# Decode attention with a parallel MLP on one core: tiles of eight heads in three slots instead of four heads in double buffers

## The chip, the cores and the metric

The kernel runs on one core of a Trainium2 chip. The metric is the device time in microseconds of one launch. A core has five engines with instruction streams of their own: PE (matmul), DVE (vector), ACT (scalar), POOL and SP; SP does no arithmetic here and issues the large loads. Engines meet only at semaphores: an instruction that waits holds up everything behind it in its own stream.

## The reference, cut to what matters

There are 8 sequences with one new token each, 32 heads of 128 and a cache of 4096 keys a head, all in bf16. With `xn` the layer norm of `x`:

```
q = xn @ wq                                   # 8 x 4096, 32 heads of 128
scores = einsum(q, k_cache) * 128**-0.5       # 8 x 32 x 4096
o = einsum(softmax(scores), v_cache)          # 8 x 32 x 128
out = x + o @ wo + gelu(layernorm(xn) @ w1 + b1) @ w2 + b2
```

K and V are 268 MB each; all weights together are some 15 MB. Every byte is used once.

## The kernel before, in words

A tile is one sequence and four heads (`HS = 4`): 4 MB of K and 4 MB of V, so there are 64 tiles. Partition `p` holds 128 consecutive keys of one head, 32 KB in one piece; 32 partitions belong to a head. K and V have two buffers each (`K_sb`, `V_sb`), and a third area `W_sb` holds in turn `wq`, the MLP's weights and `wo`.

Of a tile's 128 key columns, 40 are scored on PE (`jp_of`): groups of eight are transposed (`pe_T`, into `TR_ps`), copied out by ACT (`act_T`, into `KT_sb`) and multiplied by q (`pe_QK`). DVE scores the other 88 in four chunks (`dve_chunk`): multiply by q, add the halves, reduce. `act_S` brings PE's scores beside DVE's, `dve_max` forms one maximum, and `act_exp` takes four exps, one a head, each on that head's 32 partitions; the columns of `P_sb` that belong to other heads' partitions are zero from a memset. `pe_RS` sums the denominators, `pe_PV` runs 128 matmuls, one per key column, with V as the stationary operand, and `act_O` and `o_norm` store the tile's four heads in `oT_sb`.

The order of each engine's work is written out by hand: `at(pos, fn, ...)` notes a call with a position, the list is sorted by position and, at equal positions, by the order of the notes, and each call then appends its instructions to the streams of its engines. Tile `i` owns the positions from 100i to 100i+100, and nothing is reordered later. All five streams are replayed in full, without loops. SP's stream per tile:

```python
            if i >= 2:
                at(o - 90, load_k, i)
            if i >= 1:
                at(o + 20 if i != NQ - 2 else o + 20, load_v, i)
```

`load_k(i)` waits until tile i-2 has been scored (`kt`, `km`), `load_v(i)` until tile i-2's PV is done. At the end, heads 0 to 27 of the output are transposed into a layout that lets `wo` come in large rows (`pe_ot`, `cp_ot`, `pe_ox`, `cp_ox`); the last projection has the attention output as the stationary operand and `wo` moving (`fin_woa`, `fin_wob`). Every operation goes through one replay helper, so the profile gives L99 for nearly all of them, and tiles tell them apart.

Of the kernel before, what the change touches and what calls it, by code (L numbers as in the profile page):

```python
# [13 lines left out]
P = 128  # L14
# [127 lines left out]
def bass_parallel_sum__gqa_block_cached__mixer_channel_mlp__decode_kernel(  # L142
# [16 lines left out]
    assert DH == P and D % P == 0 and B == 8 and H % 4 == 0 and SK % P == 0  # L159
    HS = 4  # L160
# [9 lines left out]
    CHMAX = 22  # L170
    LOOP0, LOOPN = 4, 28
    NHA = H - HS
    assert NKEY == 128
    NS = 5

    def jp_of(i):
        return 64 if i == NQ - 1 else 48 if i == NQ - 2 else 40

    def chunks(i):
        jd = NKEY - jp_of(i)  # L180
        n = -(-jd // CHMAX)
        return [(jd * c // n, jd * (c + 1) // n) for c in range(n)]

    bank0 = [0]
    for i_ in range(NQ):
        bank0.append(bank0[-1] + jp_of(i_) // TPB)
    chunk0 = [0]
    for i_ in range(NQ):
        chunk0.append(chunk0[-1] + len(chunks(i_)))
    V_CUT = {NQ - 2: (0, 64, 128), NQ - 1: (0, 48, 96, 128)}  # L190
    K_CUT = {}
    WO_CUT = (0, 14, 21, 25, 27, NHA)

    x2 = A_x.rearrange("b s d -> (b s) d")
    out2 = out.rearrange("b s d -> (b s) d")

    with ExitStack() as es:
# [5 lines left out]
        K_sb = sb("K_sb", [P, 2, NKEY, DH], BF)  # L203
        V_sb = sb("V_sb", [P, 2, NKEY, DH], BF)
        W_sb = sb("W_sb", [P, DC * H * DH], BF)
        wq_sb = W_sb[:, :].rearrange("p (c n) -> p c n", c=DC)
        w1_sb = W_sb[:, 0:DC * F].rearrange("p (c n) -> p c n", c=DC)
        w2_sb = W_sb[:, DC * F:DC * F + (FB + 1) * D].rearrange("p (c n) -> p c n", n=D)
        woa_sb = W_sb[:, 0:NHA * D].rearrange("p (c n) -> p c n", n=D)
        wob_sb = W_sb[:, NHA * D:H * D].rearrange("p (h n) -> p h n", n=D)  # L210
        O_sb = W_sb[0:B, 0:NHA * DH]
        b1_sb = W_sb[0:1, DC * F + (FB + 1) * D:DC * F + (FB + 1) * D + F]
        assert DC * F + (FB + 1) * D + F <= DC * H * DH and H * D <= DC * H * DH
        KT_sb = sb("KT_sb", [P, NS, TPB, P], BF)
        Y_sb = sb("Y_sb", [P, CHMAX, DH], BF)
        Y2_sb = sb("Y2_sb", [P, 2, CHMAX, DH // 2], BF)
        Sd_sb = sb("Sd_sb", [P, 2, NKEY], F32)
        P_sb = sb("P_sb", [P, 2, NKEY, HS], BF)
# [5 lines left out]
        oX_sb = sb("oX_sb", [P, NHA, B], BF)  # L224
        x_sb = sb("x_sb", [B, D], BF)
        b2_sb = sb("b2_sb", [1, D], BF)
        xn_sb = sb("xn_sb", [B, D], BF)
        y_sb = sb("y_sb", [B, D], BF)
        st_sb = sb("st_sb", [B, 2, 16], F32)
        xT_sb = sb("xT_sb", [P, 2, DC, B], BF)  # L230
        hT_sb = sb("hT_sb", [P, FB + 1, B], BF)
        iota_i = sb("iota_i", [P, P], I32)
        ident_f = sb("ident_f", [P, P], F32)
        ident_bf = sb("ident_bf", [P, P], BF)
        ones_sb = sb("ones_sb", [1, B], BF)
        zeros_sb = sb("zeros_sb", [P, P], BF)
        mx_sb = sb("mx_sb", [P, 32], F32)
        mxT_sb = sb("mxT_sb", [P, 32], F32)
        mq_sb = sb("mq_sb", [P, 1], F32)
        nsc_sb = sb("nsc_sb", [P, 32], F32)  # L240
        mb_sb = sb("mb_sb", [P, 32], F32)
        NB_sb = sb("NB_sb", [P, 2, 32], F32)
        rs4_sb = sb("rs4_sb", [P, 2, HS], F32)
        ri4_sb = sb("ri4_sb", [P, 2, HS], F32)
        ones_f = sb("ones_f", [P, P], F32)
        resT_sb = sb("resT_sb", [P, DC * B], F32)
        out_sb = y_sb
# [3 lines left out]
        PV_ps = ps("PV_ps", [P, 2, 512], F32)  # L251
        CH_ps = ps("CH_ps", [P, 512], F32)
        ACC_ps = ps("ACC_ps", [P, 512], F32)
        TRF = TR_ps[:, :, :].bitcast(F32)
        TRB, SB_, PVB = [_Bank(), _Bank()], [_Bank(), _Bank()], [_Bank(), _Bank()]
        CHB, ACCB = _Bank(), _Bank()
        RS_ps = CH_ps[:, 0:2 * HS].rearrange("p (s h) -> p s h", h=HS)
        QT_ps = CH_ps[:, 64:64 + H * B]
        HT_ps = CH_ps[:, 64:64 + (FB + 1) * B]
        OR_ps = ACC_ps[:, :].bitcast(BF)  # L260
        FIN_ps = S_ps

        pe, dve, act, sp, pool = (_Eng(sem(f"{n}_s")) for n in ("pe", "dve", "act", "sp", "pool"))
        NPIECE = 4
        ld_k = [[_Dma(sem(f"ld_k{s}_{q}")) for q in range(NPIECE)] for s in range(2)]
        ld_v = [[_Dma(sem(f"ld_v{s}_{q}")) for q in range(NPIECE)] for s in range(2)]
        ld_x, ld_b1, ld_b2, ld_wq, ld_w1, ld_w2a, ld_w2b, ld_wob, st_a, st_b = (
            _Dma(sem(n)) for n in ("ld_x", "ld_b1", "ld_b2", "ld_wq", "ld_w1", "ld_w2a", "ld_w2b",
                                   "ld_wob", "st_a", "st_b"))
        ld_woa = [_Dma(sem(f"ld_woa{q}")) for q in range(len(WO_CUT) - 1)]  # L270
# [6 lines left out]

# [3 lines left out]
        def cuts(kind, i):  # L281
            c = (K_CUT if kind == "k" else V_CUT).get(i, (0, NKEY))
            return list(zip(c[:-1], c[1:]))

        def piece_of(kind, i, lo, hi):
            return [tk[(kind, i, q)] for q, (a, b) in enumerate(cuts(kind, i)) if a < hi and b > lo]

        def cache_src(cache, i, lo, hi):
            hq, b = divmod(i, B)
            return cache[b, hq * HS:(hq + 1) * HS].rearrange(  # L290
                "h (p j) d -> (h p) j d", j=NKEY)[:, lo:hi, :]

        def load_k(i):
            s = i % 2
            if i >= 2:
                sp.wait(tk[("kt", i - 2)], tk[("km", i - 2)])
            for q, (lo, hi) in enumerate(cuts("k", i)):
                tk[("k", i, q)] = ld_k[s][q].sig(sp.dma_start(
                    K_sb[:, s, lo:hi, :], cache_src(A_k_cache, i, lo, hi)))

        def load_v(i):
            s = i % 2
            if i >= 2:
                sp.wait(tk[("pv", i - 2)])
            for q, (lo, hi) in enumerate(cuts("v", i)):
                tk[("v", i, q)] = ld_v[s][q].sig(sp.dma_start(
                    V_sb[:, s, lo:hi, :], cache_src(A_v_cache, i, lo, hi)))

        def load_mlp():
            sp.wait(tk["q_all"])  # L310
            tk["b1"] = ld_b1.sig(sp.dma_start(b1_sb, B_b1.rearrange("(o f) -> o f", o=1)))
            tk["w1"] = ld_w1.sig(sp.dma_start(w1_sb, B_w1.rearrange("(p c) f -> p c f", c=DC)))
            tk["w2a"] = ld_w2a.sig(sp.dma_start(
                w2_sb[:, 0:FB, :], B_w2[0:FB * P, :].rearrange("(p c) n -> p c n", c=FB)))
            tk["w2b"] = ld_w2b.sig(sp.dma_start(w2_sb[0:FLAST, FB, :], B_w2[FB * P:F, :]))

        def load_woa(q):
            sp.wait(tk["ox"])
            lo, hi = WO_CUT[q], WO_CUT[q + 1]
            tk[("woa", q)] = ld_woa[q].sig(sp.dma_start(  # L320
                woa_sb[:, lo:hi, :], A_wo[0:NHA * DH, :].rearrange("(p c) n -> p c n", c=NHA)[:, lo:hi, :]))

        def load_wob():
            sp.wait(tk["ox"])
            tk["wob"] = ld_wob.sig(sp.dma_start(
                wob_sb, A_wo[NHA * DH:H * DH, :].rearrange("(h p) n -> p h n", p=P)))


        def consts_pool():
            tk["iota"] = pool.sig(pool.iota(iota_i[:, :], [[1, P]], base=0, channel_multiplier=-1))  # L330
            pool.memset(zeros_sb[:, :], 0.0)
            pool.memset(ones_sb[:, :], 1.0)
            pool.memset(mx_sb[:, :], 0.0)
            pool.memset(rs4_sb[:, :, :], 0.0)
            pool.memset(ones_f[:, :], 1.0)
            t = pool.sig(pool.memset(nsc_sb[:, :], -SCALE))
            tk["consts"] = t
            pool.wait(t)
            tk["pz"] = pool.sig(pool.memset(P_sb[:, :, :, :].rearrange("p n j h -> p (n j h)"), 0.0))

        def norm(w):
            src, dst = (x_sb, xn_sb) if w == 0 else (xn_sb, y_sb)
            st = st_sb[:, w, :]
            if w == 0:
                dve.wait(tk["x"])
            else:
                dve.wait(tk["xn"])
# [13 lines left out]
                dst[:, :], src[:, :], st[:, 12:13], st[:, 15:16], ALU.subtract, ALU.mult))  # L361

        def idents():
            dve.wait(tk["iota"])
            dve.tensor_scalar(ident_bf[:, :], iota_i[:, :], 0.0, None, ALU.is_equal)
            tk["id"] = dve.sig(dve.tensor_scalar(ident_f[:, :], iota_i[:, :], 0.0, None, ALU.is_equal))
# [14 lines left out]
        def pe_q(h0, h1):  # L381
            pe.wait(tk["wq"], tk[("xT", 0)])
            CHB.use(pe)
            for h in range(h0, h1):
# [3 lines left out]
            t = CHB.used(pe, pe.sig(last))  # L388
            if h1 == H:
                tk["q_all"] = t  # L390

        def cp_q(h0, h1):
            CHB.use(dve)
            t = CHB.used(dve, dve.sig(dve.tensor_copy(
                qT_sb[:, h0:h1, :].rearrange("p h b -> p (h b)"), QT_ps[:, h0 * B:h1 * B])))
            for h in range(h0, h1):
                tk[("q", h)] = t

        trn = [0]

        def qrep(i):
# [45 lines left out]
        def pe_QK(i, t):  # L447
# [3 lines left out]
            if t == 0:  # L451
                SB_[s].use(pe)
# [72 lines left out]
        def pe_PV(i, q):  # L525
            s = i % 2
            lo, hi = cuts("v", i)[q]
            if q == 0:
                PVB[s].use(pe)
# [279 lines left out]
```

## Time and profile before

| | |
|---|---|
| median of 3 runs | 1309.99 us (1309.28 to 1310.24) |
| span of the profiled execution | 1308.0 us |
| its own time, taken as span plus the 2.0 us by which the median is longer | 1310.0 us |
| busy: DVE / PE / ACT / POOL | 1122.7 / 677.6 / 550.6 / 48.5 us |
| moved by DMA | 553.82 MB, mean 423 GB/s |
| granted PE clock, mean | 0.568 |

The busy lines of the page count tenths of each fortieth of the span. The timeline gives start, duration, engine, operation with tile names and count, and in brackets how long the engine had been idle and what it waited for. SPq is SP's issue of a DMA.

### The profile page before, as it was taken

Reading aid. Unit: us, or ns where it says so; the run is one execution under the profiler, and the core shown is the slowest. Engines: PE = TensorE matmul, PEld = TensorE weight load, DVE = VectorE, ACT = ScalarE, POOL = GpSimd, SP = SyncE. Lnnn points to the kernel's source line nnn. Section 1 sums busy time; section 2 is a strip of 40 time slices with the busy share of each in tenths; the row PEclk is TensorE's granted clock in tenths of the full one; section 3 lists DMA queues with packets and bytes.
Section 4 is the critical chain, followed back from the end, with each engine's and each line's share of the span. In section 5 each row is a group of like instructions: output and inputs, shape, how many; then the busy total and the mean of one; then the engine's idle time right before and its main releaser. Section 6 shows DMA issues by size and latency. Waiting matters only on the chain.

```text
span 1308.0 us, 31232 instructions
## 1 busy us (share of the span) xinstructions
PE 677.6 (52%) x14035; PEld 605.4 (46%) x14035; DVE 1122.7 (86%) x1170; ACT 550.6 (42%) x1233; POOL 48.5 (4%) x139
## 2 busy tenths in 40 slices
PE   2664454454554554554544544544644544544657
PEld 1654454454444444444544544543533544544555
DVE  2898988988988988988988988988988989889873
ACT  1453453453453453443443543543533533534542
POOL 0000000000000000000000000000000000000000
PEclk9755555655555555555565555555555555555567
DMA  9999999999999999999999999999999999999996
GB/s 405 427 425 431 429 432 429 428 429 427 431 431 431 428 430 427 429 430 430 429 430 428 429 431 425 423 429 427 425 430 417 431 428 420 430 426 426 429 422 268
DMA packets 20811, 553.82 MB, mean 423 GB/s; under 512 B 2282, under 2 KB 3011, under 8 KB 3268
## 3 DMA queue, kind: packets, MB, share of 16 engines
q1 hardware_dynamic: 20642, 551.80, 98.7%
q8 instruction: 110, 1.80, 0.6%
q14 instruction: 25, 0.20, 0.0%
q10 hardware_dynamic: 34, 0.02, 0.0%
HBM read 551.80 MB, written 0.01 MB: 422 GB/s over the span
## 4 chain that ended last, share of the span: by engine, by line
DMA 64%; DVE 28%; issue 4%; PE 3%; ACT 1%; SPq 0%; DVEq 0%
DMA K_sb<-in_A_k_cache_dram 54%; DVE Y_sb L99 19%; DVE Sd_sb L99 8%; DMA V_sb<-in_A_v_cache_dram 5%; DMA W_sb<-in_A_wo_dram 3%; DMA W_sb<-in_B_w_dram 1%; PE PV_ps L99 1%; PE CH_ps L99 1%; PE TR_ps L99 1%; ACT KT_sb L99 1%; PE S_ps L99 0%; DVE ri_sb L99 0%; ACT P_sb L99 0%; PE ACC_ps L99 0%; SPq L99 0%
## 5 line engine op out<-in xcount | busy, mean ns | idle before, releaser
L99 ACT ACTIVATE KT_sb<-TR_ps 128x1024 bf16<-128x1024 bf16 x324 | 321.7, 1022 | 476.4 <-PE TR_ps L99 474.4
L99 DVE TENSOR_TENSOR Y_sb<-K_sb,qbc_sb 128x2816 bf16<-128x2816 bf16 (+2 forms) x255 | 410.5, 1610 | 108.5 <-DMA K_sb<-in_A_k_cache_dram 108.5
L99 PE MATMUL TR_ps<-ident_bf,K_sb 128*128 128x128 bf16 x2592 | 300.9, 297 | 386.8 <-DMA K_sb<-in_A_k_cache_dram 385.4
L99 PEld LDWEIGHTS TR_ps<-ident_bf,K_sb 128*128 128x128 bf16 x2592 | 240.9, 136 | 392.6 <-DMA K_sb<-in_A_k_cache_dram 391.0
L99 DVE TENSOR_REDUCE Sd_sb<-Y_sb 128x22 f32<-128x1408 bf16 (+2 forms) x255 | 412.4, 1617 | 8.7
L99 PE MATMUL PV_ps<-P_sb,V_sb 128*128 128x4 bf16 x8192 | 229.5, 166 | 19.2 <-DMA V_sb<-in_A_v_cache_dram 14.5
L99 DVE TENSOR_TENSOR Y_sb<-Y_sb 128x1408 bf16<-128x1408 bf16 (+2 forms) x255 | 231.6, 908 | 8.7
L99 PEld LDWEIGHTS PV_ps<-P_sb,V_sb 128*128 128x128 bf16 x8192 | 224.8, 104 | 22.3 <-DMA V_sb<-in_A_v_cache_dram 16.8
L99 PE MATMUL S_ps<-qrep_sb,KT_sb 128*128 128x4 bf16 x2592 | 122.9, 171 | 73.7 <-ACT KT_sb L99 69.5
L99 PEld LDWEIGHTS S_ps<-qrep_sb,KT_sb 128*128 128x128 bf16 x2592 | 101.2, 105 | 123.3 <-ACT KT_sb L99 120.3
L99 ACT ACTIVATE P_sb<-Sd_sb,NB_sb 32x128 bf16<-32x128 f32 x256 | 147.3, 575 | 12.1 <-DVE NB_sb L99 7.6
L99 ACT ACTIVATE oU_sb<-PV_ps 128x4 f32<-128x4 f32 x63 | 11.0, 174 | 219.8 <-PE PV_ps L99 219.7
L99 PE MATMUL CH_ps<-rs_sb,ones_f 128*128 128x4 f32 x128 | 36.6, 356 | 124.1 <-ACT P_sb L99 122.2
L99 PEld LDWEIGHTS CH_ps<-rs_sb,ones_f 128*128 128x128 f32 x128 | 31.0, 301 | 130.3 <-ACT P_sb L99 128.0
L99 POOL TENSOR_TENSOR oT_sb<-oU_sb,ri_sb 128x4 bf16<-128x4 f32 x63 | 30.1, 478 | 1204.2 <-ACT oU_sb L99 1169.7
L99 ACT ACTIVATION_READ_ACCUMULATOR P_sb<-Sd_sb,NB_sb 32x1 f32 x256 | 63.8, 249 | 0.0
L99 ACT ACTIVATE Sd_sb<-S_ps 32x40 f32<-32x40 f32 (+2 forms) x256 | 48.9, 191 | 3.1 <-PE S_ps L99 0.8
L99 ACT ACTIVATE qbc_sb<-TR_ps 128x128 bf16<-128x128 f32 x64 | 17.7, 277 | 24.3 <-PE TR_ps L99 22.6
L99 DVE TENSOR_REDUCE mx_sb<-Sd_sb 128x1 f32<-128x128 f32 x64 | 18.3, 286 | 6.6
L99 POOL COPY qrep_sb<-qT_sb 128x128 bf16<-128x128 bf16 x64 | 20.9, 328 | 36.8 <-PE S_ps L99 22.3
L99 PE MATMUL CH_ps<-xT_sb,W_sb 128*128 128x8 bf16 (+1 forms) x230 | 11.1, 179 | 16.2 <-DMA W_sb<-in_A_wq_dram 10.6
L99 DVE RECIPROCAL ri_sb<-CH_ps 128x4 f32<-128x4 f32 x64 | 11.1, 173 | 8.7 <-PE CH_ps L99 8.7
(63 smaller groups left out, 148.7 us busy)
## 6 DMA issues: line engine op xcount, KB each, us to landing
K_sb<-in_A_k_cache_dram SPq DMA_DIRECT2D x64, 4096.0 KB, 25.1
V_sb<-in_A_v_cache_dram SPq DMA_DIRECT2D x62, 4096.0 KB, 34.6
W_sb<-in_A_wq_dram SPq DMA_DIRECT2D x1, 5120.0 KB, 15.2
V_sb<-in_A_v_cache_dram SPq DMA_DIRECT2D x2, 2048.0 KB, 33.0
V_sb<-in_A_v_cache_dram SPq DMA_DIRECT2D x2, 1536.0 KB, 26.7
W_sb<-in_A_wo_dram SPq DMA_DIRECT2D x1, 2240.0 KB, 25.9
W_sb<-in_B_w_dram SPq DMA_DIRECT2D x1, 2160.0 KB, 17.2
W_sb<-in_B_w_dram SPq DMA_DIRECT2D x1, 2080.0 KB, 22.1
```

What stands on the lines that cost most here:

```text
L99: inst = getattr(e, name)(*a, **k)
```

## The change

A tile is now one sequence and eight heads: 8 MB of K and 8 MB of V, 32 tiles, 64 KB in one piece per partition, 16 partitions a head, 256 key columns. SBUF holds three such slots: K of even tiles (`KA`), K of odd tiles (`KB`) and one for V (`VS`); V of the last tile goes to `KA`. The weights have no area of their own: `wq`, `w1` and at the end `wo` lie in the V slot, `w2` and the small tensors of the start in `KB`. So V and K of the first tiles wait for the end of the MLP, and `wo` for the PV of tile 30.

PE scores 80 of 256 columns in ten groups with two `KT_sb` buffers. DVE scores 176 in three chunks and writes its intermediate results over K. Since heads now start at partitions that are no multiple of 32, PE's scores are taken by a product with a mask and a reduction on DVE (`dve_sel` in place of `act_S`), and each of the eight exps runs over all 128 partitions with a bias of about -1e30 where the head is another. `P_sb`, `PV_ps` and the V slot exist once. `wo` is the stationary operand in the last projection and comes in rows of 1280 B; the layout change before it is gone. PE, DVE and ACT replay tiles 4 to 29 as a loop of 13 turns of two tiles, where a wait's number is computed from the turn.

```diff
-    HS = 4
+    HS = 8
-    CHMAX = 22
-    LOOP0, LOOPN = 4, 28
-    NHA = H - HS
-    NS = 5
+    NS = 2
+    LOOP0, LOOPN = 4, 13
+    SLOT = NKEY * DH
+    KA, KB, VS = 0, 1, 2
+    WO_CUT = (0, 16, 24, 28, 30, H)
     def jp_of(i):
-        return 64 if i == NQ - 1 else 48 if i == NQ - 2 else 40
+        return 128 if i == NQ - 1 else 80
...
+    def vslot(i):
+        return VS if i < NQ - 1 else KA
...
+        S_sb = sb("S_sb", [P, 3, SLOT], BF)
+        wq_sb = part(VS, 0, DC * H * DH).rearrange("p (c n) -> p c n", c=DC)
+        w1_sb = part(VS, DC * H * DH, DC * F).rearrange("p (c n) -> p c n", c=DC)
+        wo_sb = part(VS, 0, H * D).rearrange("p (h n) -> p h n", n=D)
...
         def load_k(i):
-            s = i % 2
+            s = kslot(i)
             if i >= 2:
                 sp.wait(tk[("kt", i - 2)], tk[("km", i - 2)])
+            elif s == KB:
+                sp.wait(tk["mlp"])
+            tk[("k", i)] = ld_s[s].sig(sp.dma_start(tile[s], cache_src(A_k_cache, i)))
         def load_v(i):
+            s = vslot(i)
+            if s == KA:
+                sp.wait(tk[("kt", NQ - 2)], tk[("km", NQ - 2)])
+            elif i == 0:
+                sp.wait(tk["mlp"])
+            else:
+                sp.wait(tk[("pv", i - 1)])
+            tk[("v", i)] = ld_s[s].sig(sp.dma_start(tile[s], cache_src(A_v_cache, i)))
+        def load_wo(q):
+            sp.wait(tk[("pv", NQ - 2)])
+            lo, hi = WO_CUT[q], WO_CUT[q + 1]
+            tk[("wo", q)] = ld_wo[q].sig(sp.dma_start(
+                wo_sb[:, lo:hi, :], A_wo[lo * DH:hi * DH, :].rearrange("(h p) n -> p h n", p=P)))
...
+        def dve_chunk(i, c):
+            kt = tile[kslot(i)][:, lo:hi, :]
+            dve.wait(tk[("k", i)], tk[("qb", i)])
+            t = dve.sig(dve.tensor_tensor(
+                kt, kt, qbc_sb[:, s, :][:, None, :].to_broadcast([P, w, DH]), ALU.mult))
+            t = dve.sig(dve.tensor_tensor(kt[:, :, 0:DH // 2], kt[:, :, 0:DH // 2], kt[:, :, DH // 2:DH], ALU.add))
+            tk[("km", i)] = dve.sig(dve.tensor_reduce(Sd_sb[:, s, lo:hi], kt[:, :, 0:DH // 2], AX.X, ALU.add))
+        def dve_sel(i, f):
+            sp_ = S_ps[:, f, 0:hw * HS].rearrange("p (j h) -> p j h", h=HS)
+            t = dve.sig(dve.tensor_tensor(
+                sp_, sp_, mask_sb[:, None, :].to_broadcast([P, hw, HS]), ALU.mult))
+            tk[("s", i)] = SBK[f].used(dve, dve.sig(dve.tensor_reduce(
+                Sd_sb[:, s, j0:j0 + hw], sp_, AX.X, ALU.add)))
+        def act_exp(i):
+            act.wait(tk[("nb", i)], tk.get(("pv", i - 1)), tk.get(("rs", i - 2)))
+            for h in range(HS):
+                last = act.activation(P_sb[:, :, h], Sd_sb[:, s, :], ACT.Exp, bias=NB_sb[:, s, h:h + 1],
+                                      scale=SCALE, accum_out=rs_sb[:, s, h:h + 1])
+        def pe_PV(i):
+            v = tile[vslot(i)]
+            PVB.use(pe)
+            pe.wait(tk[("exp", i)], tk[("v", i)])
+            for j in range(NKEY):
+                last = pe.matmul(PV_ps[:, 0:HS], v[:, j, :], P_sb[:, j, :],
+                                 start=(j == 0), stop=(j == NKEY - 1))
...
         for i in range(NQ):
             o = i * Q
             last = i == NQ - 1
-            if i >= 2:
-                at(o - 90, load_k, i)
-            if i >= 1:
-                at(o + 20 if i != NQ - 2 else o + 20, load_v, i)
+            at(o - 50 if i else -700, load_k, i) if i else None
+            at(o + 50 if not last else o, load_v, i)
+            at(o - 60, qrep, i)
+            at(o - 28, pe_qbc, i)
+            at(o - 27.5, act_qbc, i)
             nt = jp_of(i) // TPB
+            w = 42.0 / nt
             for t in range(nt):
+                at(o + w * t, pe_T, i, t)
+                at(o + w * (t + 0.4), act_T, i, t)
+                at(o + w * (t + 1.5), pe_QK, i, t)
+            at(o + 2, dve_chunk, i, 0)
+            at(o + 27, dve_chunk, i, 1)
+            at(o + 54, dve_sel, i, 0)
+            at(o + 57, dve_sel, i, 1)
+            at(o + 60, dve_chunk, i, 2)
+            at(o + 85, dve_max, i)
+            at(o + Q + 15 if not last else o + 90, act_exp, i)
+            at(o + Q + 46 if not last else o + 92, pe_RS, i)
+            at(o + Q + 53 if not last else o + 94, dve_rinv, i)
+            at(o + Q + 50, pe_PV, i)
             if not last:
+                at(o + Q + 71, act_O, i)
+            at(o + Q + 75, o_norm, i)
+        o = NQ * Q
+        for q in range(len(WO_CUT) - 1):
+            at(o + q, load_wo, q)
+            at(o + 80 + q, fin_wo, q)
+        at(o + 90, fin_store)
...
+        def replay(e, n):
+            m = marks[n]
+            _replay_loop(e, engs[n].calls, m[0], m[-1], LOOPN)
```

## The prediction

> **What bounds the kernel now.** I read the slices of the span first, then the chain that ended last, then the timeline of one tile in mid-run, the last tile and the start. The slices and the DMA queues:
>
> ```profile
> DVE  2898988988988988988988988988988989889873
> ...
> DMA  9999999999999999999999999999999999999996
> GB/s 405 427 425 431 429 432 429 428 429 427 431 431 431 428 430 427 429 430 430 429 430 428 429 431 425 423 429 427 425 430 417 431 428 420 430 426 426 429 422 268
> ...
> q1 hardware_dynamic: 20642, 551.80, 98.7%
> ...
> DMA 64%; DVE 28%; issue 4%; PE 3%; ACT 1%; SPq 0%; DVEq 0%
> ```
>
> The DMA engines are busy in every slice at about 430 GB/s; DVE, at 86%, fits beside them. So the time is 551.8 MB at the queue's rate, and what matters in a change is first whether the queue ever runs dry. One tile in mid-run shows why it does not now:
>
> ```profile
> 613.55 0.33 SPq L99 DMA_DIRECT2D K_sb<-in_A_k_cache_dram  x1
> ...
> 613.92 0.43 SPq L99 DMA_DIRECT2D V_sb<-in_A_v_cache_dram  x1
> ...
> 619.38 1.89 PE L99 MATMUL TR_ps<-ident_bf,K_sb 128*128 128x128 bf16 x16 [6.15 <-DMA K_sb<-in_A_k_cache_dram]
> 620.45 1.94 ACT L99 ACTIVATE KT_sb<-TR_ps 128x1024 bf16<-128x1024 bf16 x2 [6.95 <-PE TR_ps L99]
> ...
> 625.81 0.58 ACT L99 ACTIVATE P_sb<-Sd_sb,NB_sb 32x128 bf16<-32x128 f32 x1
> ...
> 626.40 0.58 ACT L99 ACTIVATE P_sb<-Sd_sb,NB_sb 32x128 bf16<-32x128 f32 x1
> ...
> 629.09 3.58 PE L99 MATMUL PV_ps<-P_sb,V_sb 128*128 128x4 bf16 x128 [0.28 <-DMA V_sb<-in_A_v_cache_dram]
> ...
> 633.46 0.33 SPq L99 DMA_DIRECT2D K_sb<-in_A_k_cache_dram  x1
> ```
>
> Loads are issued at 613.6, and K of the tile before lands only at 619.4: PE waits for data that was queued long ago, never the queue for PE. Note the order on PE and ACT: tile i's transposes and evictions first, then exp and PV of tile i-1. That is harmless while loads run ahead.
>
> **The change, step by step.** *The order of loads.* V(i) and K(i+1) both stand at 100i+50, V(i) noted first. V(i) waits for PV(i-1), since there is one V slot; K(i+1), whose slot has long been free, stands behind that wait on SP, and nothing else loads. PV(i-1) also stands at 100i+50, behind all ten groups of tile i on PE (the last at 100i+44), and these need K(i). exp(i-1), at 100i+15, stands behind four evictions of tile i on ACT. So the work is a ring: K(i) lands, ten groups with exp(i-1) among them, PV(i-1), only then issue of V(i) and K(i+1), K(i+1) lands. From K(i)'s landing to PV(i-1)'s end the queue is empty: V(i-1) came before K(i). One turn:
>
> - Streams: 2 x 8.39 MB at 430 GB/s, 39.0 us (433 to 425 GB/s: 38.7 to 39.5). I give 64 KB rows no gain.
> - Start and landing on an empty queue. The start of the trace bounds this:
>
> ```profile
> 0.73 0.40 SPq L99 DMA_DIRECT2D W_sb<-in_A_wq_dram  x1
> 0.75 0.58 ACTq L99 DMA_DIRECT2D x_sb<-in_A_x_dram  x1
> ...
> 2.56 0.87 DVE L99 BATCH_NORM_STATS2 st_sb<-x_sb 8x6 f32<-8x320 bf16 x2 [2.56 <-DMA x_sb<-in_A_x_dram]
> ...
> 15.98 0.70 PE L99 MATMUL CH_ps<-xT_sb,W_sb 128*128 128x8 bf16 x20 [10.57 <-DMA W_sb<-in_A_wq_dram]
> ...
> 25.68 1.04 PE L99 MATMUL TR_ps<-ident_bf,K_sb 128*128 128x128 bf16 x8 [8.08 <-DMA K_sb<-in_A_k_cache_dram]
> ```
>
> x, 10 KB, takes 1.8 us; wq, 5.24 MB, takes 15.25, of which 12.2 stream: 3.0. I take 2.5, nearer to wq, which is large too.
>
> - Ten groups. The last tile of before has eight without an exp between:
>
> ```profile
> 1271.57 1.89 PE L99 MATMUL TR_ps<-ident_bf,K_sb 128*128 128x128 bf16 x16 [6.33 <-DMA K_sb<-in_A_k_cache_dram]
> ...
> 1273.72 0.38 PE L99 MATMUL S_ps<-qrep_sb,KT_sb 128*128 128x4 bf16 x8 [0.26 <-ACT KT_sb L99]
> ...
> 1280.90 0.36 PE L99 MATMUL S_ps<-qrep_sb,KT_sb 128*128 128x4 bf16 x8 [0.56 <-ACT KT_sb L99]
> ```
>
> 9.69 us for eight, 1.03 a group, so 11.7 for ten. Eight transposes take 1.04 us on an idle PE, 0.61 on a busy one; with the slowest spacing there, 1.33, it is 14. I take 12.3, as PE cools twice a turn. Two `KT_sb` buffers cost nothing: PE's order already puts QK(t-2) ahead of T(t).
> - Eight exps. They start 0.595 us apart at 128 elements. ACT's copies of 40 and 64 scores (191 and 215 ns) give 1.0 ns an element, so 0.72 at 256 and 5.8 in all. Ends: no growth 4.8, full doubling 9.5; nearest is the slope.
> - RS 0.36 and PV 256 x 28 ns (3.58 us for 128): 7.5.
> - Computed waits of the loops: no row. A plain wait to issue on SP is 0.02 to 0.05 us; some 25 on PE a turn, one or two extra instructions each, give 0 to 2.5. I take 0.7, since most are computed while the engine is busy. The 13 jumps back fall where PE, ACT and DVE wait for K.
>
> One turn: 39.0 + 2.5 + 12.3 + 5.8 + 7.5 + 0.7 = 67.8 us (ends 64.5 and 76.0) against 39.3 for two tiles before.
>
> *DVE* is off the path: its fold rows (410.5 + 231.6 + 412.4 over 64 tiles) give 33.0 per new tile; four sel operations of 320 elements at 1.07 ns + 0.1 (the reduce row) 1.8, maximum and reciprocal 1.8: 37 of 67.8. Folding in place may cost up to 30 us a tile more before DVE is late; twice the fold's time would just reach that, and DVE would be the next limit. POOL's copies (0.3 to 0.5 us) and qbc lie beside the loads. *act_S* (0.8 a tile) leaves ACT.
>
> *Start.* wq is in at 16.0; w1, w2, K0, V0, K1 are 29.6 MB, 68.8 us: K1 lands at 84.8. This needs the MLP over before K0 is in (45): q 160 x 28 ns = 4.5, MLP 14 x 0.54 = 7.6, table and gelu 2, second layer 2, over at 33.
>
> *Turns.* Thirty, to K31 at 84.8 + 30 x 67.8 = 2119.
>
> *End.* V31 follows K31 directly. Sixteen groups (17.9) with exp(30) (5.8): 23.7; DVE, whose reciprocal for tile 30 stands ahead, then does sel 2.6, the third chunk 8.1, maximum 1.5: 36; exp(31) 5.8, PV 7.5: 50; 160 `wo` matmuls of 28 ns 4.5; copy, transpose, store 2.8: 57. `wo` is issued after PV(30), at 31, and needs 14.7 at full rate, twice that if 1280 B rows halve it: 46 to 60, hidden or 5 more. The layout change that leaves cost no queue time.
>
> Span 2119 + 57 = 2176; with the 2.0 us around the span 2178, against 1310.0 for the same execution of before, whose median is 1309.99. I say 2180, 1.66 times before.
>
> **Rivals.** *A, not slower: the queue stays full.* Were K(i+1) in flight before PV(i-1) ends, a turn would be 39.0 us: 85 + 30 x 39.0 + 57 + 2 = 1314, or 1305 at the 433 GB/s seen for K0. It decides at a load issued 28 us before PV(i-1) ends. For it: loads run ahead in the trace of before, whose V has two buffers. Against: SP's order. 4%. [...]
>
> *B: PV(i-1) gets ahead of tile i's groups.* Then K's landing, fold 37, exp 5.8, PV 7.5, load 41.5 make 92 per two tiles: 85 + 30 x 46 + 59 = 1524. The order on PE speaks against it. 4%.
>
> *C: exps cost far more,* because `P_sb` is written every 16 bytes instead of every 8. If the time per exp doubles, 3.7 a turn: 2180 + 31 x 3.7 = 2295, beyond that 2400. The 575 ns at 128 elements against 277 for a dense copy of as many (`qbc_sb`) speaks for a price of strides or of the accumulator. 18%. [...]
>
> *D: computed waits cost 0.2 us each on the path,* 5.0 instead of 0.7 in each of the 26 looped tiles: 2180 + 26 x 4.3 = 2292. No row speaks to it. 14%.
>
> **How the numbers follow.** The forecast has 60%, C 18, D 14, A 4, B 4. The ends of the turn give 84.8 + 30 x 64.5 + 57 = 2079 and 84.8 + 30 x 76.0 + 62 = 2429; reaching into C and D and leaving out A, B and the far ends, 2090 to 2360. Faster 0.03 and same 0.01 (within 0.2%, about what a measurement tells apart) are A's; slower 0.96.
>
> **What would show it.** DMA slices with gaps of 28 us every 68 at about 6 tenths mean; SP waiting for `PV_ps` most of the time; PE waiting for K some 41 us a tile; exps 0.72 us apart. I am wrong if SP issues K(i+1) before PV(i-1) ends, or if exp and groups together take far from 18 us.

## The result and the profile after

The changed kernel takes 2265.47 us (2265.21 to 2265.86) against 1309.85 for the kernel before beside it: 1.730 times, interval 1.727 to 1.732. The profiled execution has a span of 2263.6 us, so 1.9 lie around it. The forecast was 2180, 85 less; the time lies inside the range of 2090 to 2360.

The lines of the page that answer to those of before, the slices of the span, the loads' queue and the chain that ended last:

```profile
DMA  9477445664446644466544665446664466644584
GB/s 413 205 297 297 186 186 223 297 296 204 185 204 296 296 204 204 185 296 296 222 197 192 278 296 241 185 203 261 296 259 185 185 259 296 259 190 199 241 371 169
...
q1 hardware_dynamic: 13904, 551.79, 57.4%
...
DMA 56%; PE 19%; ACT 19%; issue 3%; another core or an unknown queue 1%; DVE 1%; SPq 0%; ACTq 0%
```

The same 551.8 MB move, but the queue is busy for 57.4% of the span instead of 98.7%, and PE and ACT now hold 38% of the chain instead of 4%. Where the queue is empty is seen in a table of four stretches of mid-run, each cut at the landing of a K or at the issue of a V (columns: stretch, length, busy us and instructions of each engine, granted clock, DMA share, GB/s):

```profile
1102.00:1143.20 41.20, 0.10 (x1) 0.00 (x0) 7.02 (x8) 0.40 (x2) 1.52 (x2) 0.50 0.96 407
1143.20:1172.10 28.90, 18.14 (x419) 16.62 (x419) 26.94 (x13) 19.04 (x27) 0.00 (x0) 0.62 0.00 0
1172.10:1213.20 41.10, 0.06 (x1) 0.00 (x0) 7.05 (x8) 0.38 (x2) 1.59 (x2) 0.50 0.96 408
1213.20:1242.40 29.20, 18.44 (x419) 16.85 (x419) 27.00 (x13) 19.07 (x27) 0.00 (x0) 0.56 0.00 0
```

The kernel loads for 41 us with PE and ACT idle, and then computes for 29 us with no byte moving. SP's waits, in us in total, times and the longest, say whom the loads wait for (`load_v` waits for PV; the profile names `QB_ps`, the one product that PE issues right behind PV):

```profile
SPq L99 <- PE QB_ps L99: 2132.9, 31, 84.0
```

One turn in the timeline, from one landing of K to the next:

```profile
1143.25 1.89 PE L99 MATMUL TR_ps<-ident_bf,S_sb 128*128 128x128 bf16 x16 [41.15 <-DMA S_sb<-in_A_k_cache_dram]
...
1148.74 1.43 ACT L99 ACTIVATE P_sb<-Sd_sb,NB_sb 128x256 bf16<-128x256 f32 x1
...
1149.70 1.61 ACT L99 ACTIVATE P_sb<-Sd_sb,NB_sb 128x256 bf16<-128x256 f32 x1
...
1150.83 1.61 ACT L99 ACTIVATE P_sb<-Sd_sb,NB_sb 128x256 bf16<-128x256 f32 x1
...
1157.66 2.23 ACT L99 ACTIVATE KT_sb<-TR_ps 128x1024 bf16<-128x1024 bf16 x2
...
1159.04 0.38 PE L99 MATMUL S_ps<-qrep_sb,KT_sb 128*128 128x8 bf16 x8 [9.29 <-ACT KT_sb L99]
...
1165.13 6.90 PE L99 MATMUL PV_ps<-P_sb,S_sb 128*128 128x8 bf16 x256
...
1172.07 0.33 SPq L99 DMA_DIRECT2D S_sb<-in_A_v_cache_dram  x1
...
1172.44 0.43 SPq L99 DMA_DIRECT2D S_sb<-in_A_k_cache_dram  x1
...
1213.24 1.89 PE L99 MATMUL TR_ps<-ident_bf,S_sb 128*128 128x128 bf16 x16 [41.08 <-DMA S_sb<-in_A_k_cache_dram]
```

This is the ring that was forecast: K lands, the groups of its tile and the exps of the tile before, PV, and only then V and the next K. Its terms: 21.9 us from landing to PV (of which 8.9 are the eight exps, 1148.74 to 1157.66, in which PE waits 9.3 us for an eviction that stands behind them), 6.9 for PV, 41.2 from issue to landing: 70.0 us. Over tiles 2 to 29 the means are 22.1, 6.9 and 41.3, 70.4 in all.

### The profile page after: what moved, and what is told of

It reads as the page before. It is cut to its first block, busy times and chain, and to the rows that moved or that the text cites. A ratio compares the mean times of both kernels' runs of the same rounds, so it can differ in the third digit from the quotient of the medians.

```text
span 2263.6 us, 31350 instructions
## 1 busy us (share of the span) xinstructions
PE 623.4 (28%) x14000; PEld 567.7 (25%) x14000; DVE 1086.0 (48%) x662; ACT 634.0 (28%) x909; POOL 49.8 (2%) x74
## 3 DMA queue, kind: packets, MB, share of 16 engines
q1 hardware_dynamic: 13904, 551.79, 57.4%
## 4 chain that ended last, share of the span: by engine, by line
DMA 56%; PE 19%; ACT 19%; issue 3%; another core or an unknown queue 1%; DVE 1%; SPq 0%; ACTq 0%
DMA S_sb<-in_A_k_cache_dram 56%; ACT P_sb L99 12%; PE PV_ps L99 9%; ACT KT_sb L99 7%; PE TR_ps L99 7%; PE S_ps L99 3%; PE CH_ps L99 0%; SPq L99 0%; PE QB_ps L99 0%; DVE S_sb L99 0%; DVE Sd_sb L99 0%; PE ACC_ps L99 0%; ACTq L97 0%; ACT L99 0%
## 5 line engine op out<-in xcount | busy, mean ns | idle before, releaser
L99 DVE TENSOR_TENSOR S_sb<-S_sb,qbc_sb 128x7552 bf16<-128x7552 bf16 (+2 forms) x96 | 386.9, 4030 | 1053.3 <-DMA S_sb<-in_A_k_cache_dram 1053.3
L99 PE MATMUL TR_ps<-ident_bf,S_sb 128*128 128x128 bf16 (+1 forms) x2618 | 307.6, 296 | 1286.1 <-DMA S_sb<-in_A_k_cache_dram 1278.5
L99 PEld LDWEIGHTS TR_ps<-ident_bf,S_sb 128*128 128x128 bf16 (+1 forms) x2618 | 240.6, 135 | 1292.0 <-DMA S_sb<-in_A_k_cache_dram 1284.4
L99 DVE TENSOR_REDUCE Sd_sb<-S_sb 128x59 f32<-128x3776 bf16 (+2 forms) x96 | 387.0, 4031 | 3.3
L99 ACT ACTIVATE P_sb<-Sd_sb,NB_sb 128x256 bf16<-128x256 f32 x256 | 300.9, 1596 | 5.1 <-DVE NB_sb L99 5.1
L99 PEld LDWEIGHTS PV_ps<-P_sb,S_sb 128*128 128x128 bf16 x8192 | 224.5, 104 | 0.0
L99 PE MATMUL PV_ps<-P_sb,S_sb 128*128 128x8 bf16 x8192 | 222.0, 168 | 0.0
L99 PE MATMUL S_ps<-qrep_sb,KT_sb 128*128 128x8 bf16 x2608 | 126.5, 178 | 328.3 <-ACT KT_sb L99 322.4
L99 DVE TENSOR_TENSOR S_sb<-S_sb 128x3776 bf16<-128x3776 bf16 (+2 forms) x96 | 201.4, 2098 | 3.3
L99 ACT ACTIVATION_READ_ACCUMULATOR P_sb<-Sd_sb,NB_sb 128x1 f32 x256 | 128.7, 503 | 0.0
## 6 DMA issues: line engine op xcount, KB each, us to landing
S_sb<-in_B_w_dram SPq DMA_DIRECT2D x1, 2160.0 KB, 20.4
S_sb<-in_A_wo_dram SPq DMA_DIRECT2D x1, 640.0 KB, 12.3
```

The lines of the kernel that those rows point to most:

```text
L99: inst = getattr(e, name)(*a, **k)
```

## The experiments

### K ahead of V on SP

SP issues the load of the next K, whose slot is free, before it waits for the V slot. The compute streams keep their order.

```diff
-            at(o - 50 if i else -700, load_k, i) if i else None
+            at(o - 50.5, load_k, i) if i else None
```

> One position changed: SP issues K(i+1) before the wait for V(i). Theory (ring: nothing is loaded from K(i)'s landing to the end of PV(i-1), 29 us of each turn of 70): the turn falls to the stream of two 8.39 MB loads, 39.0 us; K1 at 86, K31 at 86 + 30 x 39.0 = 1256, end 64.5 later, about 1322 us (1310 to 1345). Rival (the tile of eight heads, the fold in place, masked exps, the single V slot or the loops cost the time themselves): stays above 2000 us.

Measured: 1301.84 us (1301.22 to 1302.69), 0.994 times before (0.9925 to 0.9958). Its slices and its SP waits:

```profile
DMA  9998999999999999999999999999999999999995
GB/s 412 429 428 357 445 429 431 429 436 434 430 440 428 436 434 436 432 434 438 426 440 432 432 434 434 438 426 442 430 432 436 434 436 428 442 428 434 433 427 207
```

```profile
SPq L99 <- PE QB_ps L99: 1014.8, 31, 36.9
SPq L99 <- DVE Sd_sb L99: 147.6, 30, 6.8
```

One place in SP's list is worth 963.6 us. The expectation, 1322 (1310 to 1345), was some 20 us too high: it let K1 land at 86 as in the changed kernel, but the new position puts K1 ahead of V0 too, and it lands at 66.2. From there to K31 at 1234.7 a turn takes 38.95 us, against 39.0 expected. SP still waits 1015 us for PV, but with a K in flight, so the wait costs nothing. The change as a whole was therefore not slow; the ring made by the order of two loads was.

### PV ahead of the next tile's groups

The other way to open the ring: V first as in the changed kernel, but exp, RS and PV of a tile stand in their own tile.

```diff
-            at(o + Q + 15 if not last else o + 90, act_exp, i)
-            at(o + Q + 46 if not last else o + 92, pe_RS, i)
+            at(o + 90, act_exp, i)
+            at(o + 92, pe_RS, i)
...
-            at(o + Q + 50, pe_PV, i)
+            at(o + 93, pe_PV, i)
```

> exp, denominator and PV of a tile stand right behind its maximum, ahead of the next tile's groups; SP's order is that of the changed kernel. Theory (the ring, with PV's place on PE as one link): two tiles take K's landing to the maximum 34, exps 9, PV 7.4, loads 41.2, so 92 us for two; K31 at 86 + 15 x 92 = 1466, the end 55 later, about 1520 us (1490 to 1560). Rival (only SP's order counts, or the loads are slow): over 2000 us, as in the changed kernel.

Measured: 1550.82 us (1548.69 to 1551.74), 1.184 times before (1.182 to 1.186). Its issues of V:

```profile
609.35 0.33 SPq L99 DMA_DIRECT2D S_sb<-in_A_v_cache_dram  x1
...
657.96 0.33 SPq L99 DMA_DIRECT2D S_sb<-in_A_v_cache_dram  x1
...
701.99 0.33 SPq L99 DMA_DIRECT2D S_sb<-in_A_v_cache_dram  x1
```

Two turns take 48.6 + 44.0 = 92.6 us, where rival B had worked out 92. That the two agree so closely is partly luck: from K's landing to the first exp it takes 34.5 us where B had 37 for DVE's fold, and the eight exps take 8.9 where B had 5.8. The time is 27 us over B's 1524 and inside the 1490 to 1560 expected. The same loads in the same order on SP thus cost 715 us less once PV does not stand behind the next K.

### P written densely

The eight heads' P stand one after the other, so an exp writes 256 elements in a row instead of one every 16 bytes; PV picks its column with a step.

```diff
-        P_sb = sb("P_sb", [P, NKEY, HS], BF)
+        P_sb = sb("P_sb", [P, HS, NKEY], BF)
...
-                last = act.activation(P_sb[:, :, h], Sd_sb[:, s, :], ACT.Exp, bias=NB_sb[:, s, h:h + 1],
+                last = act.activation(P_sb[:, h, :], Sd_sb[:, s, :], ACT.Exp, bias=NB_sb[:, s, h:h + 1],
...
-                last = pe.matmul(PV_ps[:, 0:HS], v[:, j, :], P_sb[:, j, :],
+                last = pe.matmul(PV_ps[:, 0:HS], v[:, j, :], P_sb[:, :, j],
```

> P is stored with the keys of one head next to each other, so the exps write densely and PV reads eight columns 512 B apart. Theory X (the scattered write makes the exp slow: 1.13 us each): dense exps of 256 take about 0.6 us (a dense copy of 128 takes 0.28, of 1024 1.02, the accumulator's read 0.25), eight save 4.2 us in each of 31 turns and at the end, some 2130 us, if PV stays at 7.0 us. Rival Y (an exp with accumulator costs 4.2 ns an element wherever it writes): exps stay at 1.13 us and the time at 2265 us.

Measured: 2092.04 us (2091.63 to 2093.48), 1.598 times before (1.595 to 1.600). First the groups of the exps and of their accumulator reads after the change (columns: count, busy us, mean ns, idle before), then the group of the exps with dense P, and two exps of that run:

```profile
L99 ACT ACTIVATE P_sb<-Sd_sb,NB_sb 128x256 bf16<-128x256 f32 x256 | 300.9, 1596 | 5.1 <-DVE NB_sb L99 5.1
...
L99 ACT ACTIVATION_READ_ACCUMULATOR P_sb<-Sd_sb,NB_sb 128x1 f32 x256 | 128.7, 503 | 0.0
```

```profile
L99 ACT ACTIVATE P_sb<-Sd_sb,NB_sb 128x256 bf16<-128x256 f32 x256 | 125.9, 496 | 5.1 <-DVE NB_sb L99 5.1
```

```profile
1130.18 0.50 ACT L99 ACTIVATE P_sb<-Sd_sb,NB_sb 128x256 bf16<-128x256 f32 x1
...
1130.68 0.49 ACT L99 ACTIVATE P_sb<-Sd_sb,NB_sb 128x256 bf16<-128x256 f32 x1
```

Same elements, same function: 0.49 us from one exp to the next instead of 1.13, and PV, which now reads P with a step, still takes 6.97 us. Eight exps cost 3.9 instead of 8.9, 5.0 less. A mean turn falls from 70.4 to 64.9, 5.5 less; the other half microsecond lies behind the exps, in the groups, which take 7.2 to PV instead of 7.7, and why is not shown. Thirty turns give 166 us, and the end behind K31's landing, with two sets of exps, is 7.9 shorter: 173 together, as measured. The expectation of 2130 was too timid: it took a dense exp to be dearer than it is.

### P written every 8 and every 4 bytes

Only the layout differs from the changed kernel: the heads lie in two groups of four, so that an exp writes every 8 bytes (the first line added), or in four groups of two, every 4 bytes (the second); exp and PV index it accordingly.

```diff
-        P_sb = sb("P_sb", [P, NKEY, HS], BF)
+        P_sb = sb("P_sb", [P, HS // 4, NKEY, 4], BF)
+        P_sb = sb("P_sb", [P, HS // 2, NKEY, 2], BF)
```

> The changed kernel with its own order of loads; only P is laid out in two groups of four heads, so an exp writes every 8 bytes instead of every 16. Theory (a step of 8 bytes costs as much as one of 16: the kernel before has 0.595 us for 128 elements at 8 bytes, 4.6 ns each, against 4.4 ns here): exps stay at 1.13 us and the time at 2265 us. [...]

> The kernel after with P in four groups of two heads, so that an exp writes every 4 bytes, where the steps of 16, 8 and 2 bytes gave 1.13, 0.65 and 0.49 us from one exp to the next. [...] If any step other than dense pays a fixed surcharge, 0.65 us and 2140.

Measured: 2139.4 us for 8 bytes and 2092.7 for 4, one run each. Two exps of the 8-byte run, and two of the 4-byte run:

```profile
1155.43 0.86 ACT L99 ACTIVATE P_sb<-Sd_sb,NB_sb 128x256 bf16<-128x256 f32 x1
...
1156.09 0.86 ACT L99 ACTIVATE P_sb<-Sd_sb,NB_sb 128x256 bf16<-128x256 f32 x1
```

```profile
1130.57 0.58 ACT L99 ACTIVATE P_sb<-Sd_sb,NB_sb 128x256 bf16<-128x256 f32 x1
...
1131.09 0.57 ACT L99 ACTIVATE P_sb<-Sd_sb,NB_sb 128x256 bf16<-128x256 f32 x1
```

So 0.49, 0.52, 0.65 and 1.13 us for steps of 2, 4, 8 and 16 bytes (0.65 is the median of its run; the two exps shown are 0.66 apart). The theory for 8 bytes did not come true: it gave 1.13 us an exp and 2265 in all, and the run is 126 us below that. Nor did the fixed surcharge for any step, with 0.65 us and 2140 at 4 bytes: these runs show none. Against the dense write an exp costs 0.03 us more at 4 bytes, 0.16 at 8 and 0.64 at 16; why it rises so is not shown.

### Without the loops

PE, DVE and ACT replay all tiles in full, with plain waits.

```diff
-            _replay_loop(e, engs[n].calls, m[0], m[-1], LOOPN)
+            _replay(e, engs[n].calls)
```

> The three loops are written out; nothing else differs. Prediction's term: computed waits cost 0.7 us a turn on the path, 26 looped tiles give 18 us: 2247 us. Rival D (0.2 us a wait, 5 us a turn): 2135 us. Rival (fully covered): 2265 us.

Measured: 2269.43 us (2267.94 to 2270.98), 1.7325 times before (1.7296 to 1.7354), an interval that overlaps that of the changed kernel. Computed waits and jumps cost nothing that shows: without them the kernel is no faster. Nor does a gain hide behind a loss from the straight streams: from K's landing to PV a mean turn takes 22.3 us without the loops and 22.1 with them, and in neither does PE stand without a cause that the profile knows. The 0.7 us a turn that the prediction gave them are not there, and rival D falls.

### K ahead of V, without the loops

Both edits together, to see the loops where the queue is full.

```diff
-            at(o - 50 if i else -700, load_k, i) if i else None
+            at(o - 50.5, load_k, i) if i else None
...
-            _replay_loop(e, engs[n].calls, m[0], m[-1], LOOPN)
+            _replay(e, engs[n].calls)
```

> K(i+1) issued first, and the three loops written out. With K first the queue is full again, so what the loops spare it should show: instruction fetch takes 0.6% of the 16 DMA engines in the kernel before and 0.2% with the loops; 0.4% of 1302 us is 5, so 1307 us. Rival (the 8 us that K first is ahead of the kernel before come from the 64 KB rows or the end alone): 1302 us.

Measured: 1321.83 us (1318.84 to 1323.39), 1.0089 times before (1.0075 to 1.0103): 20 us slower than with K first and loops, where 5 us or none had been expected. From its page (which counts the instruction queue's packets on the same 16 DMA engines), PE's waits and its timeline:

```profile
q1 hardware_dynamic: 13904, 551.79, 97.6%
q8 instruction: 109, 1.79, 0.5%
```

```profile
PE PV_ps L99 <- issue: 106.8, 39, 4.3
```

```profile
654.01 1.40 PE L99 MATMUL PV_ps<-P_sb,S_sb 128*128 128x8 bf16 x47 [3.48 <-issue]
```

PE stops inside PV's run of 256 matmuls, 39 times and for up to 4.3 us, with nothing in the profile to wait for. With the loops that line reads 20.4 us in 8 places, all of them before 260 us or after 1220, in the straight parts or the first turn of the loop, and the instruction queue moves 0.51 MB. The trace's DMA packets show what PE waits for: each of the 39 stalls ends 1.2 to 1.6 us after a packet of 16 KB of instructions has come in. In the experiment before this one, where straight streams meet a queue that is empty for 29 us of each turn, the line is missing altogether. So in these runs the stalls need both: a straight stream and a full queue. The two are not enough by themselves: the kernel before has both, and only 4.6 us of such stalls in 6 places. Its PV runs are half as long, which may be why; no run tried it. Of the 21.2 us between the two spans, the loads' own time makes 7.7 (97.6% of 1321.1 against 98.6% of 1299.9), the instruction queue 4.0 (0.5% against 0.2%), and 9.5 are idle time of the engines that is left over (the shares are rounded, by 0.7 us each at most).

### The kernel before, with PE as a loop

One thing alone is taken from the change and put into the kernel before.

```diff
-            _replay(e, pe.calls)
+            _replay_loop(e, pe.calls, marks[0], marks[-1], LOOPN)
```

> The kernel before, with one thing taken from the change: PE's stream runs as a loop too. The kernel with K first, the loops and 64 KB rows took 1301.8 us, 8 us below the kernel before, and moved 433 GB/s in mid-run where the kernel before moved 428. Theory R (the 64 KB rows give the 8 us): the kernel before shows only 4.6 us in which PE stood without a cause that the profile knows, so its loop changes nothing, 1310 us (1308 to 1312). Theory L (PE's instructions share the transfer engines with the loads, and the loop takes their bytes away): instruction bytes fall by about the 1.3 MB by which they fell in the kernel after against its straight form, which at 428 GB/s is 3 us, 1307 us, and up to all of the 8 us, 1302, if each fetch also holds a load up.

Measured: 1297.9 us (1297.3 to 1298.6), 0.9908 times before (0.9894 to 0.9922), more than either theory gave. Its queues:

```profile
q1 hardware_dynamic: 20642, 551.80, 99.2%
q8 instruction: 20, 0.33, 0.1%
```

Against the page of before (98.7% and, for 1.80 MB of instructions, 0.6%, of a span of 1308.0), the instruction queue's time falls from 7.8 us to 1.3 and that of the loads from 1291.0 to 1285.8: 11.7 of the 11.8 us by which the span is shorter (the shares are rounded, by 0.7 us each at most). In mid-run, 200 to 1200 us, it moves 432 GB/s; the kernel before moves 428 there and the one with K first 433. So of that kernel's rate nearly all is the loop's, and for 64 KB rows, with DVE and ACT in loops too, 1 GB/s is left. Here, with the queue always full, the straight form costs 12 us and, in the experiment before, 20.

### K first and dense P

```diff
-        P_sb = sb("P_sb", [P, NKEY, HS], BF)
+        P_sb = sb("P_sb", [P, HS, NKEY], BF)
...
-            at(o - 50 if i else -700, load_k, i) if i else None
+            at(o - 50.5, load_k, i) if i else None
```

> K(i+1) issued first, and P stored densely. In mid-run the queue is the limit and the exps (1.13 to 0.49 us) lie beside it: no gain there. In the last tile exp(30) and exp(31) are on the path, 5 us each; the store of the result then hangs on wo's landing behind V31 (551.8 MB at 434 GB/s, some 1286 us after the start) and 4 us of matmuls and store: 1292 us with 2 around it. Rival (exps are covered at the end too): 1302 us.

Measured: 1291.48 us (1290.84 to 1291.96), 0.986 times before (0.9845 to 0.9876): the fastest of all, and faster than the kernel before. Its slices:

```profile
DMA  9999999999999999999999999999999999999997
GB/s 399 446 424 428 424 441 427 428 439 429 431 441 429 431 441 427 433 441 427 433 439 429 433 439 429 433 437 431 431 439 431 431 437 433 431 437 433 430 430 280
```

In mid-run it is no faster than with K first alone (433 GB/s both). The 10.4 us come from the two ends. In the fourth slice the queue no longer sags (428 against 357 GB/s): the first PV ends sooner, V of tile 1 is issued at 102.0 us instead of 106.8, and K31 lands 3.2 us sooner. And the last slice moves 280 instead of 207 GB/s: from K31's landing to the end it takes 58.1 us instead of 65.2, 7.1 less, since the exps of tiles 30 and 31 lie in that tail. The 1292 expected was met, but it had put all of the gain into the tail. Against the kernel before with PE as a loop, 1297.9, this kernel is 6.4 us ahead; of its lead of 18 over the kernel before, 12 come with the loop alone.

### The tail of that kernel

To the kernel of the last experiment one edit is added: exp and RS of tile 30 stand ahead of tile 31's groups.

```diff
-            at(o + Q + 15 if not last else o + 90, act_exp, i)
-            at(o + Q + 46 if not last else o + 92, pe_RS, i)
+            at(o + Q + 15 if i < NQ - 2 else o + 90, act_exp, i)
+            at(o + Q + 46 if i < NQ - 2 else o + 92, pe_RS, i)
```

> As the dense form with K first; also exp(30) and its denominator stand ahead of tile 31's groups, so DVE's reciprocal for tile 30 no longer waits for those groups (14 us of DVE idle in the last tile). Theory (the end is set by wo's landing): at most 2 us below the dense form, 1290 us. Rival (DVE's idle time is on the path): 8 to 14 us below it, some 1280 us.

Measured: 1291.44 us (1290.7 to 1292.3), unchanged. The last PV:

```profile
1272.80 7.00 PE L99 MATMUL PV_ps<-P_sb,S_sb 128*128 128x8 bf16 x256 [5.07 <-DMA S_sb<-in_A_v_cache_dram]
```

PE now waits 5.1 us for the last V: the compute of the tail was not the limit, the loads are. Without this edit, too, the last PV starts only 0.5 us after the last V has landed.

## Why the prediction was right, and where it was wrong

The sign, the ring and the range were right; the forecast's own number was 85 us short, and one term carries that.

- **The queue and the order of loads: right.** V(i) holds up K(i+1) on SP, and the queue is empty from K's landing to PV's end. Putting K first takes 963.6 us away. Rival A had priced a queue that stays full at 1314, or 1305 at 433 GB/s; with K first it is 1301.8, and the nearness is partly luck: K1 lands 18.6 us sooner than in A's sum, and the end takes 65.2 us instead of 57.
- **Streams, start and landing: right.** 39.0 + 2.5 were forecast from issue to landing; 41.2 measured.
- **Ten groups, RS and PV: right.** 12.3 + 0.4 were forecast for groups and RS; 21.9 − 8.9 leaves 13.0. PV took 6.9, against 7.1.
- **Eight exps: wrong, the term that failed.** The slope of ACT's copies over elements gave 0.72 us an exp at 256 elements and 5.8 in all; they take 1.13 and 8.9. The slope even gave too much: at the 8-byte step of the kernel before, 256 elements take 0.65. What the term left out was the step, which the change doubles to 16 bytes and which costs 0.48 us more an exp. That is rival C's cause, with 3.1 of the 3.7 us that a doubling would have cost: the time lies 30 us under C's 2295 and 85 above the forecast. The prediction named this cause and gave it 18%; no row of before showed a 16-byte step. Its upper end for the term, 9.5, held it; that the slope's rows were nearest was no reason, for none of them had a step that doubles. By the prediction's own sign of being wrong, exp and groups together far from 18 us, this part failed: they take 21.7 in the turn shown.
- **Computed waits: wrong, and small.** 0.7 forecast, none found; rival D is out.
- **The turn:** −0.3 + 0.3 − 0.2 + 3.1 − 0.7 on 67.8 gives 70.0. Over the thirty turns (K1 landed at 86.0, K31 at 2199.1) the mean is 70.4, 79 us more than forecast in all; the start adds 1.2.
- **DVE: right.** 37 us a tile were worked out; 34 are busy, spread over 36 from K's landing, and it waits for K every turn. Folding in place, for which up to 30 us were allowed, cost nothing that shows.
- **What the prediction did not see:** that the straight instruction streams cost the kernel before 12 us. It asked of the loops only what their waits cost. In the changed kernel that gain cannot show, since its queue is empty for two fifths of the time (busy 57.4%; 2265.5 us with the loops, 2269.4 without); with K first, at 98.6%, the loops are worth 20 us.
- **The end: mechanism right, size wrong mainly by the same term.** 57 was forecast, 64.5 measured. The groups with exp(30) are over some 4.5 us later than forecast, 3.1 of it the exps', and DVE, whose reciprocal of tile 30 stands ahead, idles until then; exp(31) adds another 3.6, PV and the rest are 0.6 shorter:

```profile
2227.75 0.21 DVE L99 RECIPROCAL ri_sb<-CH_ps 128x8 f32<-128x8 f32 x1 [13.52 <-PE CH_ps L99]
...
2239.90 1.43 ACT L99 ACTIVATE P_sb<-Sd_sb,NB_sb 128x256 bf16<-128x256 f32 x1 [5.10 <-DVE NB_sb L99]
...
2249.76 6.97 PE L99 MATMUL PV_ps<-P_sb,S_sb 128*128 128x8 bf16 x256
...
2256.59 4.41 PE L99 MATMUL ACC_ps<-oT_sb,S_sb 128*128 128x8 bf16 x160
```

The projection (the last line) starts without a wait for `wo`, which is hidden, as the lower of the two cases had it. With 1.2 from the start, 79 from the turns and 7.5 from the end, 2178 becomes 2266.

## What to carry to other kernels

When loads are issued by one in-order stream, write down for each load what it waits for and which load stands behind it: a load whose slot is free must not stand behind one that waits for compute, above all where that compute stands behind work on data that has just landed, since nothing is then loaded while it computes (29 us of each 70 here, 963.6 us in all). Check the write step of each ACT instruction when a tile's layout changes, since the step can cost more than the elements do (an exp of 256 took 0.49 us dense and 1.13 with a 16-byte step). Where the DMA queue is the bound, count the instruction bytes as traffic too, and try a loop on the engine with the most instructions (PE's loop took 1.80 MB of them to 0.33 and the time down by 12 us).

## What the runs showed of the hardware that was not expected

- An exp of 256 elements with an accumulator took 0.49, 0.52, 0.65 and 1.13 us at write steps of 2, 4, 8 and 16 bytes. Its accumulator read differs in the profile too: 0.19, 0.18, 0.26 and 0.50 us.
- A straight PE stream stalled 39 times for some 2.7 us on average (106.8 us in all) when the DMA queue was full, and not at all when the queue had gaps of 29 us a turn. Each stall ended 1.2 to 1.6 us after a fetch of 16 KB of instructions. The packet of a fetch takes 1.0 us with the full queue and 1.1 with the gaps, so the difference is not in its transfer; where it lies is not shown.
- In the kernel before, PE shows only 4.6 us of such stalls, and its loop still gave 12 us: the loss lay in the DMA engines' time, 6.5 us of fetches and 5.2 us of loads that ran slower beside them. Why the loads are slower beside 90 fetches is open.
- The kernel before's exps are 0.595 us apart at 128 elements on 32 partitions and 8 bytes, nearly as much as the 0.65 for 256 elements on 128 partitions: most of that row was no price per element, unless more partitions make an exp cheaper. What it is was not tried.
